# Loading the first half of a block's q and k by head parity, so that one full-width transpose turns two heads

## The chip, the cores and the metric

The kernel runs on one core of one Trainium2 chip. The metric is the device time of one execution in microseconds (us), as a median of several runs. The profile gives a second number, the span of the profiled execution on the core, which is about 1.8 us shorter than the time of the same run (225.7 against 227.5).

## The reference

A decayed linear attention in blocks feeds a gated feed-forward layer. Cut to what matters:

```python
# attention, per batch and head; the reference uses blocks of 64, the kernel blocks of 128
intra = (qb @ kb.T * Dmask) @ vb                  # Dmask[i, j] = lam ** (i - j), lower triangle
inter = (qb * lam_pow) @ kv_state
out[block] = intra + inter
kb_dec = kb * rev_pow                             # "decayed k"
kv_state = lam ** block * kv_state + kb_dec.T @ vb
# feed-forward on x = out, tokens x (heads * head_dim)
y = (sigmoid(x @ w_gate) * (x @ w_val)) @ w_out
```

The sizes are 4 batch elements, 8 heads, 768 positions, head dimension 64, feed-forward width 1536. With blocks of 128 positions there are six blocks, called block 0 to block 5 below.

## The kernel before

TensorE needs q and k with the head dimension on the partitions, so each head's 128 x 64 tile is transposed. Block 0 and half of block 1 are transposed by TensorE, the other half of block 1 and all later blocks by transposing transfers. Two heads share a 128-partition result. Their pairing is not free: for state and mask layouts used from block 1 on, heads `h` and `h + 2` belong together.

```python
# load(): block 1. First half (batch 0, 1) in head order, second half by parity
if n == 1 and c != "v":
    if b0 == 0:
        nc.gpsimd.dma_start(out=lst[n][:, 0]..., in_=src[b0:b1, :, sl, :]...)
    else:
        for e in range(2):
            nc.gpsimd.dma_start(out=lst[n][:, 1]...[:, e], in_=src[b0:b1, e::2, sl, :]...)
    continue
# [cut]
def transpose(out, x, b, g):                       # two half-width transposes for one pair of heads
    for u in range(2):
        nc.tensor.transpose(out[half(u)], x[:, b, head(g, u), :], ident)
# [cut]
def piece_t(n, bp):                                # block 1, first half: q, then k
    # [cut]
    for i in range(2):
        for g in range(HP):
            transpose(tq[:, g // 2, i, g % 2, :], q1, i, g)
    scale(n, bp, tq)                               # VectorE: times the decay table lamq
    for i in range(2):
        for g in range(HP):
            transpose(tk[:, g // 2, i, g % 2, :], k1, i, g)
    nc.scalar.copy(KS[n, bp], tk)
# [cut]
def make_lamq():                                   # VectorE, not touched by the change
    for u in range(2):
        nc.vector.tensor_copy(lp[us]..., lam_bc[us, :]...)        # 64 x 4
    # seven tensor_tensor products that double the table
    nc.vector.tensor_copy(lamq, lp)                               # 128 x 512
# [cut]  the order in which GpSimd issues loads, and its products between them
load(1, "qk", 0, 2); load_gv(5, GW); load(1, "v", 0, 2); load(1, "qk", 2, 4); load(1, "v", 2, 4)
fade(); make_kd(1)                                 # decayed state, decayed k of block 1
for i in range(3): load_wo(i, NFT // 3)            # output weights
load(2, "qkv", 0, B)                               # block 2; then transposing transfers on SyncE
```

## Time and profile before

| | before |
|---|---|
| time, first three runs | 227.68 us (227.13 to 227.74) |
| span of the profiled execution | 225.7 us |
| TensorE busy | 218.7 us, 97% |
| TensorE waits after 16 us | one of 0.42 us, at 74.41 us |

These lines are from the page of the kernel before: busy time by engine, the clock that TensorE was granted in 40 slices of the span (9 is 90% or more), and the engines on the chain of work that ended last.

```profile
PE 218.7 (97%) x1766; PEld 114.7 (51%) x1766; DVE 106.2 (47%) x194; ACT 79.1 (35%) x150; POOL 77.0 (34%) x74
...
PEclk9999999999999999999999999999999999999999
...
PE 66%; DMA 20%; POOL 9%; SPq 2%; issue 1%; DVE 0%; POOLq 0%
```

The kernel is bound by TensorE nearly everywhere, but the chain leaves TensorE for transfers (20% of the span) and GpSimd (9%). The next lines are that chain in order of time (start, length, what).

```profile
28.96 10.41 DMA kb<-in_k_dram
39.44 2.05 POOL kd L379 x2
41.49 2.24 POOL WO L111 x3
43.74 1.12 POOL qb L78
44.86 13.62 DMA qb<-in_q_dram
58.54 5.03 SPq L242
63.66 10.70 DMA KR<-kb
75.03 2.69 PE po L492 x12
```

Read from the bottom: the output products after 75 us follow block 2's first scores, which needed block 2's transposed k (`KR`), which needed the transposing transfer of q before it, which needed block 2's q, whose load was issued after the output weights, after the decayed k of block 1, after the load of block 1's k. TensorE's timeline (start, length, line, output and inputs, count, idle time before and who ended it) shows where that chain meets TensorE:

```profile
31.15 1.03 PE L435 MATMUL vp<-XT,WV 128*128 128x512 bf16 x4
32.10 0.64 PE L225 MATMUL tq<-ident,qb 128*64 128x128 bf16 x16
32.57 0.61 PE L225 MATMUL tk<-ident,kb 128*64 128x128 bf16 x16
33.12 1.04 PE L429 MATMUL gp<-XT,WG 128*128 128x512 bf16 x4
...
74.41 0.62 PE L309 MATMUL sp<-QS,KR 64*128 64x128 bf16 x16 [0.42 <-DMA KR<-kb]
```

At 74.41 TensorE waited 0.42 us for `KR`. And GpSimd's timeline shows the issues and products that the change touches:

```profile
19.76 1.16 POOL L86 DMA_DIRECT2D qb<-in_q_dram  x1 [1.17 <-DMA WG<-in_moe_w_gate_dram]
20.96 1.14 POOL L86 DMA_DIRECT2D kb<-in_k_dram  x1
...
35.93 1.90 POOL L373 TENSOR_TENSOR kd<-kb,kds 128x1024 bf16<-128x1024 bf16 x1
39.44 2.05 POOL L379 TENSOR_TENSOR kd<-kb,kds 128x512 bf16<-128x512 bf16 x2 [1.62 <-DMA kb<-in_k_dram]
```

### The profile page before, as it was taken

How to read it: one execution, taken by the hardware profiler on the slowest of the kernel's cores; microseconds unless marked ns; L12 is line 12 of the kernel's file. 1: busy time of each engine (PE TensorE's matmuls, PEld its weight loads, DVE VectorE, ACT ScalarE, POOL GpSimd, SP SyncE). 2: the span in 40 equal slices, each digit the busy share in tenths (PEclk: the TensorE clock that was granted, in tenths of full speed). 3: DMA queues.
4: the chain of work that ended last, by engine and by line, in shares of the span. 5: the costliest groups of instructions: out<-in, count | busy, mean ns of one | idle time of the engine just before them, and what ended most of it. 6: DMA issues, size and time to landing. Idle time of an engine off the chain costs nothing.

```text
span 225.7 us, 4301 instructions
## 1 busy us (share of the span) xinstructions
PE 218.7 (97%) x1766; PEld 114.7 (51%) x1766; DVE 106.2 (47%) x194; ACT 79.1 (35%) x150; POOL 77.0 (34%) x74
## 2 busy tenths in 40 slices
PE   7699999999999999999999999999999999999994
PEld 2355454888854455444445444446444445444443
DVE  7898647585422622435742345742334840333300
ACT  5454234344422225333115333225333225333221
POOL 8987657983294007940005950000000000000000
PEclk9999999999999999999999999999999999999999
DMA  8999999999999994999621999921820012100022
GB/s 117 154 173 196 188 176 154 143 181 172 156 127 149 229 205 131 167 151 147 24 96 46 148 157 143 66 95 50 180 54 0 0 49 93 49 0 0 0 93 97
DMA packets 105718, 25.71 MB, mean 114 GB/s; under 512 B 95842, under 2 KB 102754, under 8 KB 105698
## 3 DMA queue, kind: packets, MB, share of 16 engines
q0 software_dynamic: 81232, 13.90, 93.0%
q1 hardware_dynamic: 23426, 11.28, 23.4%
q10 hardware_dynamic: 1040, 0.26, 0.5%
q8 instruction: 14, 0.23, 0.5%
q14 instruction: 6, 0.05, 0.1%
HBM read 28.31 MB, written 6.29 MB: 153 GB/s over the span
## 4 chain that ended last, share of the span: by engine, by line
PE 66%; DMA 20%; POOL 9%; SPq 2%; issue 1%; DVE 0%; POOLq 0%
PE po L492 22%; PE gp L429 18%; PE vp L435 18%; DMA qb<-in_q_dram 6%; DMA WV<-in_moe_w_val_dram 5%; DMA KR<-kb 5%; DMA kb<-in_k_dram 5%; SPq L242 2%; PE sp L309 2%; POOL WG L103 2%; PE op L321 2%; POOL WV L103 2%; POOL vb L97 2%; PE po L481 1%; POOL kb L97 1%; PE op L333 1%
## 5 line engine op out<-in xcount | busy, mean ns | idle before, releaser
L438 DVE TENSOR_TENSOR ht<-sg,vp 128x512 bf16<-128x512 bf16 x54 | 37.1, 687 | 65.8 <-PE vp L435 65.8
L492 PE MATMUL po<-WO,ht 128*128 128x512 bf16 x276 | 61.9, 379 | 0.0
L429 PE MATMUL gp<-XT,WG 128*128 128x512 bf16 x216 | 55.5, 379 | 0.0
L435 PE MATMUL vp<-XT,WV 128*128 128x512 bf16 x216 | 55.4, 379 | 0.0
L432 ACT ACTIVATE sg<-gp 128x512 bf16<-128x512 f32 x54 | 32.2, 597 | 59.1 <-PE gp L429 59.1
L492 PEld LDWEIGHTS <-ht 128*128 128x128 bf16 x276 | 26.2, 98 | 31.0
L435 PEld LDWEIGHTS <-WV 128*128 128x128 bf16 x216 | 21.1, 98 | 25.5
L429 PEld LDWEIGHTS <-WG 128*128 128x128 bf16 x216 | 20.7, 98 | 24.8
L495 ACT COPY ob<-po 128x512 f32<-128x512 f32 x23 | 13.5, 586 | 52.7 <-PE po L492 50.9
L213 DVE TENSOR_TENSOR MT<-sp,mask 128x512 bf16<-128x512 f32 x40 | 25.1, 682 | 7.1 <-PE sp L309 7.1
L394 POOL TENSOR_TENSOR sd<-Sb,dec 128x512 f32<-128x512 bf16 x8 | 8.1, 1035 | 40.1 <-DVE Sb L420 40.0
L464 PE MATMUL gp<-XT,WG 128*128 128x256 bf16 x96 | 14.4, 273 | 0.0
L470 PE MATMUL vp<-XT,WV 128*128 128x256 bf16 x96 | 14.4, 273 | 0.0
L474 DVE TENSOR_TENSOR ht<-sg,vp 128x256 bf16<-128x256 bf16 x24 | 10.0, 420 | 8.6 <-PE vp L470 8.6
L467 ACT ACTIVATE sg<-gp 128x256 bf16<-128x256 f32 x24 | 9.2, 384 | 13.0 <-PE gp L464 11.8
L97 POOL DMA_DIRECT2D vb<-in_v_dram x10 | 12.8, 1281 | 2.5 <-DMA kb<-in_k_dram 1.0
L385 POOL TENSOR_TENSOR kd<-kb,kds 128x1024 bf16<-128x1024 bf16 x6 | 11.3, 1904 | 5.8 <-DMA kb<-in_k_dram 5.8
L420 DVE TENSOR_TENSOR Sb<-cp,sd 128x512 bf16<-128x512 f32 x8 | 5.2, 686 | 15.5 <-PE cp L413 15.5
L348 ACT CAST XT<-op 128x512 bf16<-128x512 f32 x19 | 9.9, 598 | 2.1 <-PE op L321 2.0
L464 PEld LDWEIGHTS <-WG 128*128 128x128 bf16 x96 | 9.2, 98 | 1.7 <-issue 0.2
L470 PEld LDWEIGHTS <-WV 128*128 128x128 bf16 x96 | 9.4, 98 | 1.1
L78 POOL DMA_DIRECT2D qb<-in_q_dram x8 | 9.4, 1182 | 0.0
(87 smaller groups left out, 160.0 us busy)
## 6 DMA issues: line engine op xcount, KB each, us to landing
out_dram<-ob SPq DMA_DIRECT2D x21, 256.0 KB, 2.5
kb<-in_k_dram POOLq DMA_DIRECT2D x11, 256.0 KB, 11.1
qb<-in_q_dram POOLq DMA_DIRECT2D x9, 256.0 KB, 10.0
vb<-in_v_dram POOLq DMA_DIRECT2D x4, 512.0 KB, 14.6
WO<-in_moe_w_out_dram POOLq DMA_DIRECT2D x3, 512.0 KB, 10.0
WG<-in_moe_w_gate_dram POOLq DMA_DIRECT2D x5, 256.0 KB, 9.1
WV<-in_moe_w_val_dram POOLq DMA_DIRECT2D x5, 256.0 KB, 9.7
qb<-in_q_dram POOLq DMA_DIRECT2D x4, 128.0 KB, 8.8
```

Source lines behind the costliest of these rows:

```text
L97: nc.gpsimd.dma_start(out=lst[n][:, b0:b1], in_=src[b0:b1, :, sl, :].rearrange("b h s d -> s (b h) d"))
L213: nc.vector.tensor_tensor(out=out.rearrange("p (e x) c -> p e x c", e=2), in0=x.rearrange("p (e x) c -> p e x c", e=2), in1=mask.rearrange ...
L385: nc.gpsimd.tensor_tensor(out=KD[n][:, e], in0=K[n][:, e], in1=kds[:, e::2].unsqueeze(1).unsqueeze(3).to_broadcast([128, B, HP, D]), op=AL ...
L429: nc.tensor.matmul(gp, lhsT=WG[:, mt, fs], rhs=x[:, mt, :], start=(mt == 0), stop=(mt == NMT - 1))
L432: nc.scalar.activation(sg, gp, AF.Sigmoid)
L435: nc.tensor.matmul(vp, lhsT=WV[:, mt, fs], rhs=x[:, mt, :], start=(mt == 0), stop=(mt == NMT - 1))
L438: nc.vector.tensor_mul(HT[n, ft], sg, vp)
L464: nc.tensor.matmul(gp[:, cs], lhsT=WG[:, mt, fs], rhs=x[:, mt, cs], start=(mt == 0), stop=(mt == NMT - 1))
L470: nc.tensor.matmul(vp[:, cs], lhsT=WV[:, mt, fs], rhs=x[:, mt, cs], start=(mt == 0), stop=(mt == NMT - 1))
L474: nc.vector.tensor_mul(HT[n, ft][:, cs], sg[:, cs], vp[:, cs])
L492: nc.tensor.matmul(po, lhsT=HT[n, ft][:, tt * 128:(tt + 1) * 128], rhs=WO[:, ft, :], start=(ft == 0), stop=(ft == NFT - 1))
L495: nc.scalar.copy(ob, po)
```

## The change

The intent is to halve the count of block 1's TensorE transposes. If the first half of block 1's q and k is loaded with even heads first and odd heads after them, heads `h` and `h + 2` lie side by side, and one full-width 128 x 128 transpose turns both. The decayed k must then be written in the same layout. The diff, cut to its core:

```diff
 load():
-                if b0 == 0:
-                    nc.gpsimd.dma_start(out=lst[n][:, 0]..., in_=src[b0:b1, :, sl, :]...)
-                else:
-                    for e in range(2): ...
+                for e in range(2):
+                    nc.gpsimd.dma_start(
+                        out=lst[n][:, b0 // 2].rearrange("p (e x d) -> p e x d", e=2, d=D)[:, e],
+                        in_=src[b0:b1, e::2, sl, :].rearrange("b y s d -> s (b y) d"))
 piece_t():
-        for i in range(2):
-            for g in range(HP):
-                transpose(tq[:, g // 2, i, g % 2, :], q1, i, g)
+        def turn(out, x):
+            for e in range(2):
+                for i in range(2):
+                    for g in range(2):
+                        nc.tensor.transpose(out[:, e, i, g, :],
+                                            x[:, e, i, 2 * g:2 * g + 2, :]..., ident)
+        turn(tq, q1)
         scale(n, bp, tq)
+        turn(tk, k1)
 make_kd():                                        # [cut] one product of the first half becomes two
+            for bp in range(NB2):
+                for e in range(2):
+                    nc.gpsimd.tensor_tensor(out=ko[:, e], in0=ki[:, e], in1=kds[:, e::2]..., op=ALU.mult)
```

More of the change, by code (lines that the diff above doesn't have):

```diff
@@ L84, in load @@
                     lst[n] = qkv.tile([128, 2, B * H * D // 2], BF16, tag=c + "b", name=c + "b")
-                if b0 == 0:
+                for e in range(2):
                     nc.gpsimd.dma_start(
-                        out=lst[n][:, 0].rearrange("p (x d) -> p x d", d=D),
-                        in_=src[b0:b1, :, sl, :].rearrange("b h s d -> s (b h) d"))
-                else:
-                    for e in range(2):
-                        nc.gpsimd.dma_start(
-                            out=lst[n][:, 1].rearrange("p (e x d) -> p e x d", e=2, d=D)[:, e],
-                            in_=src[b0:b1, e::2, sl, :].rearrange("b y s d -> s (b y) d"))
+                        out=lst[n][:, b0 // 2].rearrange("p (e x d) -> p e x d", e=2, d=D)[:, e],
+                        in_=src[b0:b1, e::2, sl, :].rearrange("b y s d -> s (b y) d"))
                 continue
@@ L221, in head @@
         return 4 * (g % 2) + 2 * u + g // 2
-    def transpose(out, x, b, g):
-        for u in range(2):
-            nc.tensor.transpose(out[half(u)], x[:, b, head(g, u), :], ident)
     QS, KS, MT, XT, KD = {}, {}, {}, {}, {}
@@ L285, in piece_t @@
             return
-        q1, k1 = (x[1][:, 0].rearrange("p (b h d) -> p b h d", b=2, h=H) for x in (Q, K))
+        q1, k1 = (x[1][:, 0].rearrange("p (e b y d) -> p e b y d", e=2, b=2, y=HP) for x in (Q, K))
         tq = ps_at.tile([128, 2, 2, 2, C], BF16, name="tq", tag="ps")
         tk = ps_at.tile([128, 2, 2, 2, C], BF16, name="tk", tag="ps")
-        for i in range(2):
-            for g in range(HP):
-                transpose(tq[:, g // 2, i, g % 2, :], q1, i, g)
+        def turn(out, x):
[3 more added lines that the diff above has]
+                        nc.tensor.transpose(out[:, e, i, g, :],
+                                            x[:, e, i, 2 * g:2 * g + 2, :].rearrange("p y d -> p (y d)"), ident)
+        turn(tq, q1)
         scale(n, bp, tq)
-        for i in range(2):
-            for g in range(HP):
-                transpose(tk[:, g // 2, i, g % 2, :], k1, i, g)
+        turn(tk, k1)
         KS[n, bp] = trsb.tile([128, 2, 2, 2, C], BF16, tag="KS", name="KS")
@@ L372, in make_kd @@
             KD[n] = kdp.tile([128, 2, B * H * D // 2], BF16, tag="kd", name="kd")
-            nc.gpsimd.tensor_tensor(
-                out=KD[n][:, 0].rearrange("p (b h d) -> p b h d", b=2, h=H),
-                in0=K[n][:, 0].rearrange("p (b h d) -> p b h d", b=2, h=H),
-                in1=kds.unsqueeze(1).unsqueeze(3).to_broadcast([128, 2, H, D]), op=ALU.mult)
-            ko, ki = (x[n][:, 1].rearrange("p (e b y d) -> p e b y d", e=2, b=2, y=HP) for x in (KD, K))
-            for e in range(2):
-                nc.gpsimd.tensor_tensor(
-                    out=ko[:, e], in0=ki[:, e],
-                    in1=kds[:, e::2].unsqueeze(1).unsqueeze(3).to_broadcast([128, 2, HP, D]), op=ALU.mult)
+            for bp in range(NB2):
+                ko, ki = (x[n][:, bp].rearrange("p (e b y d) -> p e b y d", e=2, b=2, y=HP) for x in (KD, K))
+                for e in range(2):
+                    nc.gpsimd.tensor_tensor(
+                        out=ko[:, e], in0=ki[:, e],
+                        in1=kds[:, e::2].unsqueeze(1).unsqueeze(3).to_broadcast([128, 2, HP, D]), op=ALU.mult)
             return
@@ L398, in kdh @@
     def kdh(n, b, h):
-        if n == 1 and b < 2:
-            return KD[n][:, 0].rearrange("p (b h d) -> p b h d", b=2, h=H)[:, b, h]
         if n == 1:
-            return KD[n][:, 1].rearrange("p (e b y d) -> p e b y d", e=2, b=2, y=HP)[:, h % 2, b - 2, h // 2]
+            return KD[n][:, b // 2].rearrange("p (e b y d) -> p e b y d", e=2, b=2, y=HP)[:, h % 2, b % 2, h // 2]
         return KD[n][:, b, h, :] if n == 0 else KD[n][:, h % 2, b, h // 2, :]
```

## The prediction

> **What bounds the kernel now.** TensorE. By engine, it is busy 218.7 us of a 225.7 us span (97%) at full granted clock in all 40 slices. After 16 us its timeline lists one idle time: 0.42 us at 74.41 us, before the first score matmuls of block 2, ended by the landing of block 2's transposed k. The chain of waits leads back from there through transfers: block 1's last k load but one (landed 39.37), two GpSimd products for the decayed k (39.44 to 41.49), the issues of the output weights and of block 2's loads, block 2's q landing at 58.5, the two transposing transfers (58.54, 63.66; landed 74.36). So up to 74 us two chains are nearly tied: TensorE and the load queue.
>
> **What the change does, costed.**
> - TensorE: 32 half-width transposes become 16 full-width ones. Their count halves, their time does not. In the timeline the half-width ones start in pairs about 2 ns apart, a pair each 55.9 ns; block 0's full-width ones start each 55.5 ns. The Trainium skill, "TensorE: Matmul & The Clock Gate", Part 3, says that small matmuls on different column groups run at the same time; this trace agrees. 16 pairs cost what 16 full ones do: 0.9 us. What may go is the switch of shapes: 155 ns lie between the last pair and the next full matmul, against 56 ns after a full transpose in block 0. Estimate: 0.05 to 0.15 us saved.
> - Loads: two more issues (1.15 us each become two of 0.87), 1.2 us more of GpSimd between 19.8 and 34 us. Bytes and packet size (128) stay. The queue is full: loads land 8 to 11 us after issue, in order. The already split second half landed at intervals of 0.93, 0.91, 0.90, 0.78 us, the unsplit first half of 1.91 and 1.48, so splitting costs the queue nothing visible. An issue waits for the transfer eight before it; eight half transfers still cover 7 us. Landings should move by under 0.3 us.
> - Decayed k: one product of 1.90 us becomes two of 1.05, but GpSimd then waited 1.62 us for the k load anyway. Hidden.
>
> **On the critical path.** TensorE's saving before 74 us only lengthens the wait for block 2's transposed k, unless the loads also land earlier. A later k load of block 1 passes on one for one. Net: 0 to 0.15 us gain, disturbed by a few tenths of transfer timing; at most some 0.5 us could be had if the transfers came that much earlier.
>
> **Predicted:** 227.55 us, 226.8 to 228.4 in 8 of 10. Chances: faster by over 2% 0.02, within 2% 0.95, slower by over 2% 0.03.
>
> **What the profile would show.** (1) 16 full-width transposes, about 55 ns apart, in about 0.9 us. (2) First-half q and k as four issues, the last landing within 0.3 us of 32.07. (3) Four decayed-k products of 1.05 us; the third still waits for its load, near 39.4 us. (4) One TensorE wait at about 74.4 us, 0.4 to 0.6 us long, ended by the transposed k. (5) The same 151 us from there to the end.
>
> **What would make it wrong.** The two extra issues starve the load queue, so that block 1's k and then block 2's q and k land over 1 us later: the wait at 74 us grows by as much. Or the first k lands after TensorE has finished q: a stall near 32.5 us, of which 0.4 us is absorbed at 74. Or the transposing transfers collide differently with the output weights' load (40 to 45 us) and shift block 2's landing.

## More of the kernel before

The 32 half-width transposes of block 1 run from 32.10 to the next matmul at 33.12, 1.02 us. The first of them starts 0.96 us (unrounded) after the first of the four 512-column matmuls before it; four at the usual spacing of 0.216 us take 0.86, so about 0.09 us were lost before the group, too little for the profile to list as a wait.

## The result, and the profile after

| | before | after |
|---|---|---|
| median of six runs each | 227.14 us | 227.25 us |
| range | 226.60 to 227.74 | 226.68 to 227.53 |
| ratio | | 0.9999, 95% interval 0.9977 to 1.0021 |

The time is the same. Two of the same lines of the page of the kernel after (the clock's line has not changed):

```profile
PE 217.9 (97%) x1728; PEld 115.2 (51%) x1750; DVE 106.5 (47%) x194; ACT 79.1 (35%) x150; POOL 78.4 (35%) x77
...
PE 91%; DVE 3%; DMA 3%; issue 2%; ACT 1%; DVEq 0%; POOLq 0%
```

The chain of the whole execution is now TensorE's for 91%. Its timeline shows why: the transposes are 16, they take 0.89 us by the unrounded starts (32.66 to 33.56), they start 0.86 us after the first of the four matmuls before them (0.96 before), and before block 2's scores there is no wait.

```profile
31.80 1.03 PE L425 MATMUL vp<-XT,WV 128*128 128x512 bf16 x4
32.66 0.61 PE L285 MATMUL tq<-ident,qb 128*128 128x128 bf16 x8
33.11 0.61 PE L285 MATMUL tk<-ident,kb 128*128 128x128 bf16 x8
33.56 1.03 PE L419 MATMUL gp<-XT,WG 128*128 128x512 bf16 x4
...
74.35 0.62 PE L304 MATMUL sp<-QS,KR 64*128 64x128 bf16 x16
```

Note that the transposes began 0.56 us later than in the trace before, and that block 2's scores began at nearly the same time all the same. GpSimd's timeline has two issues each for the first q and k, and two products of about 1.02 us for one of 1.90:

```profile
19.54 1.82 POOL L86 DMA_DIRECT2D qb<-in_q_dram  x2 [0.62 <-DMA WG<-in_moe_w_gate_dram]
21.81 0.87 POOL L86 DMA_DIRECT2D kb<-in_k_dram  x1 [0.45 <-DMA WG<-in_moe_w_gate_dram]
23.16 0.87 POOL L86 DMA_DIRECT2D kb<-in_k_dram  x1 [0.47 <-DMA WV<-in_moe_w_val_dram]
...
35.51 2.04 POOL L371 TENSOR_TENSOR kd<-kb,kds 128x512 bf16<-128x512 bf16 x2
39.06 2.05 POOL L371 TENSOR_TENSOR kd<-kb,kds 128x512 bf16<-128x512 bf16 x2 [1.51 <-DMA kb<-in_k_dram]
```

The added issues and products are there, and the second pair of products still waits for the k load (1.51 us idle). Two things did not fit the prediction: the wait at 74 us was gone, with the transposed k landing at 73.13 instead of 74.36 us, and something before 32 us had cost 0.56 us. Either the change moved the transfers, or two executions of one kernel differ by that much.

### The profile page after: what moved, and what is told of

The parts are those of the page before. It is cut to its first block, busy times and chain, and to the rows that moved or that the text cites. A ratio compares the mean times of both kernels' runs of the same rounds, so it can differ in the third digit from the quotient of the medians.

```text
span 225.7 us, 4250 instructions
## 1 busy us (share of the span) xinstructions
PE 217.9 (97%) x1728; PEld 115.2 (51%) x1750; DVE 106.5 (47%) x194; ACT 79.1 (35%) x150; POOL 78.4 (35%) x77
## 4 chain that ended last, share of the span: by engine, by line
PE 91%; DVE 3%; DMA 3%; issue 2%; ACT 1%; DVEq 0%; POOLq 0%
PE po L482 27%; PE gp L419 21%; PE vp L425 20%; PE gp L454 5%; PE vp L460 5%; PE sp L304 3%; PE gp L433 3%; PE op L316 3%; DMA kb<-in_k_dram 3%; PE op L328 1%; PE po L471 1%; PE cp L403 1%; DVE MT L206 1%; DVE lp L194 1%; DVE ht L446 1%
## 5 line engine op out<-in xcount | busy, mean ns | idle before, releaser
L425 PE MATMUL vp<-XT,WV 128*128 128x512 bf16 x211 | 54.4, 379 | 0.0
```

The costliest lines, as they stand in the source:

```text
L425: nc.tensor.matmul(vp, lhsT=WV[:, mt, fs], rhs=x[:, mt, :], start=(mt == 0), stop=(mt == NMT - 1))
```

## The experiments

Ten runs followed, two of them repeats, each with one profiled execution and timed against the kernel before on the same chip. They came in three batches on three chips, so the table below compares traces across chips. Ratios are to the kernel before unless another is named. The table collects what all twelve traces say. "First k" is the landing of block 0's first k load. "VectorE wait" is how much later than the matmul spacing of 0.216 us the fourth value product of block 0 began, near 24 us. "Transposes" is their start, and the time from there to the next matmul. "Tr. k" is the landing of block 2's transposed k, "scores" the start of block 2's scores. All are in us.

| trace | first k | VectorE wait | transposes | tr. k | scores | span |
|---|---|---|---|---|---|---|
| before | 7.43 | 0.01 | 32.10, 1.02 | 74.36 | 74.41 | 225.72 |
| before_again | 7.55 | 0.45 | 32.58, 1.02 | 73.42 | 74.39 | 225.71 |
| after | 7.82 | 0.33 | 32.66, 0.89 | 73.13 | 74.35 | 225.67 |
| after_again | 7.49 | 0.13 | 32.10, 0.89 | 73.32 | 73.78 | 225.10 |
| t_only | 7.23 | 0.38 | 32.15, 0.89 | 73.43 | 73.84 | 225.15 |
| l_only | 7.24 | 0.58 | 32.46, 1.02 | 73.07 | 74.28 | 225.59 |
| before_x6 | 7.43 | 0.67 | 32.71, 5.48 | 73.54 | 79.00 | 230.30 |
| after_x6 | 7.46 | 0.73 | 32.71, 5.36 | 72.23 | 78.86 | 230.18 |
| pe_minus | 7.64 | 0.01 | 30.42, 2.09 | 73.57 | 73.62 | 224.95 |
| l_split | 7.34 | 0.04 | 31.92, 0.89 | 78.86 | 78.91 | 232.30 |
| lamq_act | 7.57 | 0.00 | 32.12, 0.89 | 73.30 | 73.80 | 225.13 |
| q_first_lamq | 7.18 | 0.00 | 31.72, 0.89 | 71.90 | 73.41 | 224.71 |

One number is not in the table. By the unrounded starts, the first transpose begins 0.309 us after the matmul before it in all four traces with half-width transposes (before, before_again, l_only, before_x6), and 0.215 to 0.216 us after it in all eight with full-width ones. The change thus saves 0.09 us before the group besides the 0.12 us (1.017 less 0.893) of the transposes' column, 0.22 us in all.

### Both kernels again: before_again and after_again

Theory A: the two chains are nearly tied and vary from run to run. Theory B, the rival: the change moved the transfers. Nothing is edited.

> The kernel before, unchanged, against itself. Theory A (two nearly tied chains that jitter from run to run): ratio 1.000 within the interval, but the landing of block 2's transposed k differs from the first trace's 74.36 us by up to 1.5 us and TensorE's start on block 1's transposes differs from 32.10 us by up to 0.6 us, although no instruction changed. Theory B (the change itself moved the transfers 1.2 us earlier, as the trace after shows with a landing at 73.13): this repeat again lands at 74.4 +- 0.2 and again shows a wait of 0.4 to 0.5 us there.

> The kernel after, unchanged. Theory A: time ratio 1.000 +- 0.003; the landing of block 2's transposed k anywhere from 73 to 75 us; transposes of block 1 again 0.90 us from first start to the next matmul. Theory B: landing again at 73.1 +- 0.2, no wait before block 2's score matmuls.

Measured: before_again 227.18 us, ratio 0.999 (0.9968 to 1.0013); after_again 226.96 us, ratio 0.9982 (0.9963 to 1.0001). Theory B falls: the unchanged kernel before, profiled once more, lands the transposed k at 73.42 us and has no wait there. It has one elsewhere, in TensorE's timeline:

```profile
24.72 1.02 PE L443 MATMUL gp<-XT,WV 128*128 128x512 bf16 x4 [0.29 <-DVE ht L456]
...
74.39 0.62 PE L309 MATMUL sp<-QS,KR 64*128 64x128 bf16 x16
```

So the profile of the kernel before from which I predicted was the exception, not the rule: in before_again, after, after_again, t_only and l_only the transposed k lands 0.4 to 1.2 us before TensorE gets to it. In that one trace the transposing transfer of block 1's k landed 4.8 us after its issue (40.22 to 45.00), against 3.2 us in before_again (40.23 to 43.40) and after (39.87 to 43.02), and the output weights landed some 1.5 us later than in before_again. But block 2's last q load was then only 0.17 us late (58.48 against 58.31). Most of the 0.94 us by which its transposed k was late came in the last step: the transposing transfer of that k took 10.70 us from issue to landing, against 9.79 in before_again. Nor does a slow transfer of block 1's k suffice: in after_x6 it took 4.5 us, and block 2's transposed k landed at 72.23. What made the last step slow stays open.

### The transposes alone: t_only

The kernel before with full-width transposes of its old layout. The experiment pairs neighbouring heads instead of `h` and `h + 2`, and its result is wrong (relative error 0.36). Whether one transpose could pick `h` and `h + 2` from the old layout, without moving the heads at the load, no run shows.

```diff
-        for u in range(2):
-            nc.tensor.transpose(out[half(u)], x[:, b, head(g, u), :], ident)
+        nc.tensor.transpose(out, x[:, b, 2 * g:2 * g + 2, :].rearrange("p h d -> p (h d)"), ident)
```

> Full-width transposes alone, from the old load layout, so adjacent heads are paired and the result is wrong on purpose. Both theories of the transposes: 16 at 55.5 ns, block from first start to the next matmul 0.90 us instead of 1.02. If the halved count were worth half the time (rival): 0.5 us. Whole time: same within 0.3%.

Measured: 227.01 us, ratio 0.998 (0.9959 to 1.0001). The block takes 0.89 us for 1.02: 0.13 us less (0.124 unrounded), not half. The gap before it is 0.216 us, not 0.309.

### The loads alone: l_only

The kernel after with half-width transposes (result right).

```diff
-                        nc.tensor.transpose(out[:, e, i, g, :], x[:, e, i, 2 * g:2 * g + 2, :]..., ident)
+                        for u in range(2):
+                            nc.tensor.transpose(out[half(u), e, i, g, :], x[:, e, i, 2 * g + u, :], ident)
```

> Parity loads and parity decayed k alone, half-width transposes kept; result right. If splitting the first q and k costs the load queue nothing: first k landed at 32.0 +- 0.4, third decayed-k product waits for its load as before, whole time same within 0.3%. If the two extra issues cost their 1.2 us of GpSimd (rival): decayed k ends 1.2 us later and block 2's transposed k lands 1.2 us later than before. Transposes 1.02 us.

Measured: 227.41 us, ratio 0.9997 (0.9978 to 1.0015). The first half's k landed at 31.31 us and the transposed k at 73.07, no later than in either trace of the kernel before (32.07 and 31.55; 74.36 and 73.42). The two extra issues and the extra products are hidden. The gap before the transposes is 0.309 us again, so it goes with the half-width transposes and not with the loads.

### The disputed cost by itself: before_x6 and after_x6

Each group of transposes is done six times into the same tiles, which multiplies its cost and leaves the result right.

```diff
+        for _ in range(6):
             turn(tq, q1)          # and the same around turn(tk, k1); in before, around its loops
```

> Kernel before, each group of half-width transposes done six times into the same tiles (result right). If a pair of half-width transposes costs 55.9 ns (theory): block 1.02 + 80 pairs x 0.0559 = 5.5 us, whole time +4.5 us (+2.0%), as the load queue has 0.3 to 1.2 us of slack in five of six traces and none of it is needed. If each half-width one cost 55 ns by itself (rival): block 9.8 us, +8.9 us.

> Kernel after, each group of full-width transposes done six times (result right). Theory: 80 more x 0.0557 = +4.45 us, block 5.35 us; so after_x6 minus before_x6 is again only -0.1 to -0.15 us, the switch between shapes, which is paid once. Rival (halving the count halves the time): after_x6 is 4.4 us faster than before_x6.

Measured: 231.90 us, ratio 1.0204 (1.0177 to 1.0230), and 231.70 us, ratio 1.0194 (1.0170 to 1.0218). TensorE's timeline of before_x6, then of after_x6:

```profile
32.71 2.87 PE L225 MATMUL tq<-ident,qb 128*64 128x128 bf16 x96
35.42 2.85 PE L225 MATMUL tk<-ident,kb 128*64 128x128 bf16 x96
38.20 1.04 PE L431 MATMUL gp<-XT,WG 128*128 128x512 bf16 x3
```

```profile
32.71 2.84 PE L285 MATMUL tq<-ident,qb 128*128 128x128 bf16 x48
35.39 2.84 PE L285 MATMUL tk<-ident,kb 128*128 128x128 bf16 x48
38.07 1.03 PE L421 MATMUL gp<-XT,WG 128*128 128x512 bf16 x3
```

192 half-width transposes took 5.48 us, 96 full-width ones 5.36. The extra five rounds cost the same, 4.47 us by the unrounded starts (5.484 - 1.017 and 5.360 - 0.893): 55.8 ns (4.467 us / 80) for a pair of half-width transposes and for one full-width transpose. What the change saves is paid once per group: 0.09 us in the gap before it, 0.02 us between its first two pairs (80 ns for 56), and 0.10 us after it. That the cost stays the same agrees with the Trainium skill, "TensorE: Matmul & The Clock Gate", Part 3, by which small matmuls in different column groups of the array run at the same time; the two of a pair start 3 to 4 ns apart here (the prediction says about 2). The leftover agrees with "TensorEngine Tiling (Array Packing)", Key Properties, by which a change of the tiling mode drains TensorE: in the trace before, the last pair and the next full matmul start 155 ns apart, after the last full-width transpose of the trace after it is 55 ns. That the drain is these gaps is my reading: t_only and l_only show that the gaps come and go with the half-width transposes, but no run isolates a drain.

The runs show a second thing. The extra 4.47 us arrive in the span almost whole: 230.30 - 225.71 is 4.59 us for before_x6 over before_again, of which 0.22 us are a longer VectorE wait and -0.12 an earlier first k. So TensorE's time at 32 us is on the critical path, in the normal execution, and is not swallowed at 74 us.

### Less work for TensorE: pe_minus

The kernel after without one of block 0's twelve gate and value tiles, 1.73 us of TensorE (wrong, relative error 0.15).

```diff
-    gv(0, 8)
+    HT[0, 8] = HT[0, 7]
```

> Kernel after without one of the twelve gate and value tiles of block 0 (wrong on purpose), which takes 1.73 us off TensorE before block 2. Theory (TensorE first, the load queue 0.3 to 1.0 us behind it): TensorE reaches block 2's score matmuls 1.73 us earlier and then waits 0.7 to 1.4 us for the transposed k, landing at 73.1 to 73.6 us; net gain only 0.4 to 1.0 us. If TensorE alone bound (rival 1): -1.73 us, no wait. If the load queue bound (rival 2, my prediction's chain): 0 to -0.1 us, wait of 1.7 us or more.

Measured: 226.79 us, ratio 0.9978 (0.9954 to 1.0002). TensorE's timeline:

```profile
30.42 0.67 PE L285 MATMUL tq<-ident,qb 128*128 128x128 bf16 x8
31.42 0.40 PE L285 MATMUL tk<-ident,kb 128*128 128x128 bf16 x4 [0.33 <-DMA kb<-in_k_dram]
32.27 0.40 PE L285 MATMUL tk<-ident,kb 128*128 128x128 bf16 x4 [0.46 <-DMA kb<-in_k_dram]
...
73.62 0.62 PE L304 MATMUL sp<-QS,KR 64*128 64x128 bf16 x16 [0.25 <-DMA KR<-kb]
```

The net gain over the kernel after was 0.16 to 0.72 us of span (224.95 against 225.10 and 225.67), where 0.4 to 1.0 was expected, and the interval of the times just includes no gain. Part of the saving was lost, as the theory has it, but most of the loss was not where I had put it. The saved 1.73 us met a wall already at the transposes, which took 2.09 us instead of 0.89 because the two k loads had not landed; a second, shorter wait followed at 74 us. The queue that brings block 1 and block 2 is a close second to TensorE in two places.

### More and smaller loads: l_split

The kernel after with each q and k load of block 1 split once more, by batch element: 16 issues for 8.

```diff
                 for e in range(2):
-                    nc.gpsimd.dma_start(out=...[:, e], in_=src[b0:b1, e::2, sl, :]...)
+                    for b in range(2):
+                        nc.gpsimd.dma_start(out=...[:, e, b], in_=src[b0 + b, e::2, sl, :]...)
```

> Kernel after with every q and k load of block 1 split once more, one per batch element: 16 issues for 8, the same bytes (result right). Theory that splitting is free only while eight transfers in flight cover the issue and queue time: issues of about 0.75 us each now take longer than the 0.46 us that a quarter transfer takes in the queue, so the queue runs dry; last k of block 1 lands 1.5 to 4 us later, block 2's transposed k as much, the wait before block 2 is 1 to 3 us, whole time +0.5 to +1.5%. Rival (splitting is free whatever the size): last k at 39.4 +- 0.5, whole time same.

Measured: 233.76 us, ratio 1.0305 (1.0258 to 1.0351), slower, and by more than twice the most that I had expected. GpSimd's timeline, then TensorE's waits (who, for whom, total us, times, longest):

```profile
38.57 0.74 POOL L87 DMA_DIRECT2D kb<-in_k_dram  x1 [1.06 <-DMA vb<-in_v_dram]
39.62 1.15 POOL L93 DMA_DIRECT2D vb<-in_v_dram  x1 [0.31 <-issue]
...
42.86 4.05 POOL L372 TENSOR_TENSOR kd<-kb,kds 128x512 bf16<-128x512 bf16 x4
```

```profile
PE sp L305 <- DMA KR<-kb: 3.1, 1, 3.1
PE sp L305 <- DMA HBk<-kb: 2.0, 1, 2.0
```

An issue here takes 0.74 us against 0.87 for twice the bytes and 1.15 for four times, and waits for the transfer eight before it. The last v issue ended at 40.77 us (33.84 before), the decayed k at 46.92 (41.49 before), and the transposed k landed at 78.86. Around 30 to 32 us the transfers moved 68 GB/s, against 190 in after; but the last k load landed only 1.9 us later than in after (41.72 against 39.80), and GpSimd, still busy with its issues, came to the decayed k without waiting for it. So what delayed the rest was in the main the time of the issues and of their waits. One split was free and the next one was not; TensorE paid 2.01 and 3.06 us, and then lost more (153.39 us from block 2's scores to the end, for 151.32): during 80 to 82 us it was granted 0.50 of its clock, with 0.82 and 0.83 in the two-microsecond windows around it. "TensorE: Matmul & The Clock Gate", in Why this matters for your kernels, warns of idle gaps over about 3 us for this reason; in l_split the drop followed the gap of 3.06 us. It is one case, and no run tests it by itself.

### What made the start of the transposes vary: lamq_act and q_first_lamq

In the table, subtract the first k landing and the VectorE wait from the start of the transposes: for the eleven traces with block 0's work intact this leaves 24.48 to 24.66 us. The two terms explain the start within 0.1 us, and what remains is mostly the gap before the group: the four half-width traces lie at 24.58 to 24.66, the seven full-width ones at 24.48 to 24.55. Both terms stem from before the first changed matmul. The change does add load issues near 20 to 24 us, though, so it could act on the VectorE wait: with the first loads unsplit (before, before_again, t_only, before_x6) it was 0.01 to 0.67 us, with them split 0.01 to 0.73, so no difference shows. The VectorE wait is made by three copies in `make_lamq`: it equals, in each of the first ten traces, what they took over 0.15, 0.17 and 0.43 us, to within 0.05 us. VectorE's timeline of l_only, then GpSimd's issues there:

```profile
20.70 0.53 DVE L190 COPY lp<-lam_bc 64x4 f32<-64x4 f32 x2
21.26 1.85 DVE L194 TENSOR_TENSOR lp<-lp 128x4 f32<-128x4 f32 x7
23.14 0.81 DVE L197 CAST lamq<-lp 128x512 bf16<-128x512 f32 x1
```

```profile
20.20 0.87 POOL L86 DMA_DIRECT2D qb<-in_q_dram  x1 [0.30 <-DMA WV<-in_moe_w_val_dram]
21.51 0.87 POOL L86 DMA_DIRECT2D kb<-in_k_dram  x1 [0.43 <-DMA WG<-in_moe_w_gate_dram]
22.86 0.87 POOL L86 DMA_DIRECT2D kb<-in_k_dram  x1 [0.47 <-DMA WV<-in_moe_w_val_dram]
```

The copies (0.53 for 0.32 us, 0.81 for 0.43) began while GpSimd issued a load. The Trainium skill, "SBUF — State Buffer", Who interferes with whom, says that copies and casts on VectorE can run in modes that use a port pair shared with GpSimd; the stretched copies agree. The seven products of two tensors (1.84 to 1.86 us in every trace) overlapped issues too and never grew. The edit moves the copies to ScalarE, and q_first_lamq besides issues block 2's q and k ahead of the output weights:

```diff
-            nc.vector.tensor_copy(lp[us]..., lam_bc[us, :]...)
+            nc.scalar.copy(lp[us]..., lam_bc[us, :]...)           # at the first gate tile's place
-        nc.vector.tensor_copy(lamq, lp)
+    nc.scalar.copy(lamq, lp)                                      # after sigm(0, 4, g4)
 q_first_lamq also:
-    for i in range(3): load_wo(i, NFT // 3)
-    load(2, "qkv", 0, B)
+    load(2, "qk", 0, B)
+    for i in range(3): load_wo(i, NFT // 3)
+    load(2, "v", 0, B)
```

> Kernel after, with three copies that make the decay table (two of 64x4 elements, one of 128x512) moved from VectorE to ScalarE; result right. In the ten traces so far TensorE waits 0.01 to 0.73 us at 24 us for a VectorE product, and each time just by what the three copies took over 0.15, 0.17 and 0.43 us; they are long where GpSimd issues a load at the same time. Theory (VectorE's copies are held up by GpSimd's load issues, its products of two tensors are not): that wait is below 0.05 us in this kernel, the products that make the table keep their 167 to 426 ns, whole time 0.3 us less than after on average (ratio to before about 0.998, at the edge of what five rounds resolve). Rival (VectorE is simply behind): the wait stays 0 to 0.7 us.

> The kernel lamq_act, and block 2's q and k are issued ahead of the output weights; result right. Theory (load queue a close second): block 2's transposed k lands at 60 to 68 us instead of 73.3, so the rare wait before block 2 cannot occur; TensorE's path is untouched, so the time is that of lamq_act within 0.1%. If the output weights now land after 63.5 us, a new wait appears before the first output product. Rival (the load queue sets the time): 0.5 us or more below lamq_act.

Measured: lamq_act 226.84 us, ratio 0.9987 (0.9969 to 1.0005); q_first_lamq 226.79 us, ratio 0.9982 (0.9966 to 0.9997). VectorE's, then TensorE's timeline of lamq_act:

```profile
21.03 1.84 DVE L197 TENSOR_TENSOR lp<-lp 128x4 f32<-128x4 f32 x7
22.89 0.69 DVE L448 TENSOR_TENSOR ht<-sg,gp 128x512 bf16<-128x512 bf16 x1
```

```profile
23.48 1.03 PE L435 MATMUL gp<-XT,WG 128*128 128x512 bf16 x4
24.35 1.03 PE L435 MATMUL gp<-XT,WV 128*128 128x512 bf16 x4
```

The products still take their 1.84 us, with an issue running beside them, and the value product follows the gate product with no wait. The rival (VectorE is simply behind) falls only in part: moving the copies also takes 0.75 us of work off VectorE, so this run alone could not tell; that the wait equals the stretch of the copies, trace by trace, is what decides. The gain in time is not clear of zero for lamq_act (0.13% against the kernel before, where about 0.2% was expected). In q_first_lamq the transposed k landed at 71.90 us, not at 60 to 68 as I had expected: block 2's q landed 9 us earlier (49.26), but its transposing transfers of q and k shared the time with the output weights and block 2's v, and the issue of the k one alone took 6.8 us. The slack before block 2 grew to 1.5 us all the same. This version is 0.18% faster than the kernel before with an interval that just leaves zero out, one of ten such intervals; against the kernel after it was not timed in the same rounds. Against lamq_act of the same rounds it gained nothing (226.79 and 226.84 us), as the theory has it and not the rival.

## Why the prediction was right

The time was right: 227.55 predicted, 227.25 measured, and "within 2%" with 0.95. Two terms of its reasoning were not: the path, and the size of TensorE's saving. Point by point:

- **The transposes cost the same by pairs.** Right, and shown by the sixfold runs: 55.8 ns for a pair and for a full one. But the saving was put too low: 0.05 to 0.15 us was forecast from the switch of shapes after the group (155 against 56 ns), which gave 0.10 us as forecast. The gap before the group (309 against 216 ns) and the slow second pair were left out; with them it is 0.22 us.
- **The loads cost nothing visible.** Right (l_only). The text said that the last of the first k would land within 0.3 us of 32.07; it landed at 31.60 and 31.16, and in the repeat of the kernel before at 31.55. The tolerance was too narrow for one trace.
- **The decayed k is hidden.** Right: GpSimd still waits 1.51 us for the k load.
- **"TensorE's saving before 74 us only lengthens the wait for block 2's transposed k".** Wrong in the normal execution. That wait existed in the one trace that I had, and later only where I took work off TensorE (pe_minus) or split the loads too far (l_split). TensorE comes last, and the 0.22 us pass through: after_again is 0.60 us shorter in span than before_again, of which the first k gives 0.06, the VectorE wait 0.33, the gap before the transposes 0.09 and the transposes 0.12. That the wrong path did not spoil the number was luck: both readings give nearly nothing, since 0.22 us is 0.1% of the time, and the interval of six runs is 0.2% either way.
- **Point 4, a wait of 0.4 to 0.6 us at 74.4**: not seen after the change, nor in the second trace before it. **Point 5, the same time from there to the end**: 151.32 us in both.
- **The failure that I had named, a starved load queue**, is real and is one split away: l_split cost 3.05%.

So the change is worth about 0.22 us of TensorE, shown in the traces, and no resolvable amount of time. What varies between executions is larger: the first k's landing spread over 0.64 us and the VectorE wait over 0.73.

## What to carry to other kernels

Count array time, not instructions: two half-width transposes on different column groups already ran at once, so joining them saved the gaps around the group and not half the work; look for such gaps before a group as well as after it, also where the profile lists no wait. Before a wait of half a microsecond is made the hinge of a prediction, profile the same kernel once more, because a chain that leads by less than the run-to-run spread may be another one next time. A split of a load that is free once is not free twice: compare the issue's own time and the number of transfers in flight with the time a piece spends in the queue.

## What the Trainium skill lacked or had wrong

- "SBUF — State Buffer", Who interferes with whom, says of VectorE in a mode that uses the shared port pair: whichever of it and GpSimd issues first has the pair for its whole instruction, and the other is fully blocked. The traces agree that copies are held up by load issues and that products of two tensors are not. But the block was not for the whole issue. It reached 0.63 us (0.80 for 0.17 us, in before_x6); copies begun in an issue's first 0.18 us were not delayed, nor those begun in its last 0.18; the ones delayed had begun 0.29 us or more into it and ended as if they had started about 0.2 us before its end (l_only: the issue ended at 23.73 us, the cast at 23.96, 0.43 us after 23.53).
- "DMA: Bandwidth & Descriptors", Anatomy of one DMA, calls the time of descriptor generation small and variable, and Latency and other measured facts has one figure for a load issued by GpSimd, about 1 us to the first byte. In these traces one load issue takes GpSimd 0.74, 0.87 and 1.15 us for 64, 128 and 256 KB landed in 64-element rows, so halving a load does not halve its issue: the 8 issues of block 1's q and k took 7.0 us in after, the 16 of l_split 12.3.
- "TensorEngine Tiling (Array Packing)", Key Properties, names a drain when the mode changes, without a size. Removing two-head packing from one group of transposes saved 0.22 us here: 0.09 before the group, 0.02 at its second pair, 0.10 after it. That these gaps are the drain is a reading.
